# Pooled attention in front of two feed-forward stages: the order in which queries lie in the tiles, and when a pair's first queries are turned

## The chip, the cores and the metric

One Trainium2 chip, one core of it. Time is the device time of one execution in microseconds (us), lower is better; the runs give a median. A profile is one execution of the same program with the hardware profiler on.

## The reference, cut to what matters

```python
# q, k, v: (2 batches, 8 heads, 1152, 64) f32
q_pool = q.reshape(B, H, S // 2, 2, D).mean(axis=3)            # 576 queries a head
scores = matmul(q_pool, k.transpose(0, 1, 3, 2)) / sqrt(D)
attn = exp(scores - max(scores, -1)); attn /= attn.sum(-1) + 1e-9
x = matmul(attn, v)  ->  x of (1152 tokens, 512)                # token = batch * 576 + query
h = x @ w_in;  x = (h * tanh(softplus(h))) @ w_out              # 512 -> 2048 -> 512 ("Mish")
P = exp(x @ w_gate - max); 8 rounds: rows and columns of P scaled to sums (Sinkhorn)
out[n] = sum over 8 experts e of P[n, e] * (relu(x[n] @ w1[e]) @ w2[e])
```

Nothing after the attention mixes tokens except the column sums of P, which take all of them. So tokens may lie in any order on the chip, if the output rows go to their places.

## The kernel before, in words

Every matmul operand is split in two halves of fewer bits, a high and a low one (`split_hi`, L72, and `split_lo`, L80), and products are summed from them.

The attention goes over 8 pairs of heads (`p`), four in each batch. A pair has 2 x 576 = 1152 queries, 9 tiles of 128 (`QTL`): tiles 0 to 3 are of the first head, 5 to 8 of the second, and the middle tile 4 (`MID`) has the last 64 of the first head and the first 64 of the second. One step of the loop at L685 is one tile (`g`, with `t = g mod 9` inside pair `p`). In step `g` TensorE is given, in this order: the scores of tile `g` (`scores`, L443), one turning of keys if there is one, the turning of the exponentials of tile `g-3` (`transposes`, L521), up to 9 products of attention and values (`run_av`, L588), and the other turnings of keys or queries. ScalarE's exponential of tile `g` (`exps`, L462) stands after all of the step's copies.

- Scores come in one PSUM buffer. VectorE takes them to `e` (L458, three buffers), ScalarE makes the exponentials in place, and a DMA copies them to `er` (`hand_over`, L474, two buffers), issued in step `g+1`. TensorE turns them in step `g+3`. The buffer of `er` is free when tile `g-2` has been turned; the buffer of `e` when its copy has landed.
- Queries: `load_q` (L340) loads a pair's, `split_q` (L363) on GpSimd adds the two that are pooled, scales and splits them in four operations (`q0` to `q3`), `trans_q` (L428) turns four tiles at once, with the high half on partitions 0 to 63 and the low half on 64 to 127. ScalarE copies them to `qT`; `swap` (L423) makes a second copy with the two halves exchanged, by two DMAs inside SBUF. A tile's scores are two products for each third of the keys: with the first copy, then with the swapped one. The middle tile has its own buffers `qz` (`middle`, L403), with zeros where the other head's would be.
- `PREP` (L607) says in which `t` GpSimd does which split for pairs 1 and later (`PREP0` for pair 0): `q0` to `q3` of the next pair's queries; `k00`, `k01` the two halves of the next pair's first keys; `k10`, `k11` of its second; `v00` to `v11` of this pair's values. `TURN` (L612) says in which `t` the turnings stand: `"q": (7, 1, 2)` means that the next pair's tiles 0 to 3 are turned in step 7, its tiles 4 to 7 in its own step 1, tile 8 in its step 2.
- `loads` is a list of DMAs that a step adds to, and that SyncE issues at the start of the next step, in the order of the list and ahead of that step's `hand_over`. A swap gets onto it with its turning, a load of keys, values or queries when the last split of the ones before is put down, since the raw buffers are single.
- The row sums of a pair are turned, written to a row in DRAM and read back broadcast over the 64 partitions of each head (`turn_sums`, L485; `back` in step 4 of the next pair). GpSimd multiplies the attention's output `xs` by them and splits it (`split_x`, L575) at the end of that step 4, and `v10`, `v11`, `k10` and `k11` stand behind this on GpSimd.
- The attention's output is made in four groups of queries (`GROUPS`, L508: 256 and 320 of the first head, 320 and 256 of the second); `evac` (L561) adds its two halves into `xs`.

After the attention come the Mish stage, the gate, and the experts (`down`, L1175, sums into `oacc` by token tiles in the order `TILES`; in the last group each tile's rows go out by DMA, the last tile's in two halves of the columns).

Of the kernel before, what the change touches and what calls it, by code (L numbers as in the profile page):

```python
# [8 lines left out]
F32 = mybir.dt.float32  # L9
F32R = mybir.dt.float32r  # L10
# [3 lines left out]
AF = mybir.ActivationFunctionType  # L14
ALU = mybir.AluOpType
# [8 lines left out]
def pool_attention_mish_sinkhorn_kernel(  # L24
# [12 lines left out]
    nc = tc.nc  # L37
# [253 lines left out]
    with ExitStack() as actx:  # L291
# [48 lines left out]
        def load_q(p, part=slice(0, QTL)):  # L340
            b, hp, h0 = heads(p)
            if part.start == 0:
                raws["q", p] = q_p.tile([P, QTL, 2, D], F32, tag="qraw", name=f"qraw{p}")
            src = q[b, h0:h0 + 2].rearrange("h (s r) d -> (h s) r d", r=2)
            nc.sync.dma_start(
                out=raws["q", p][:, part], in_=src.rearrange("(t p) r d -> p t r d", p=P)[:, part])

        def split_kv(p, j, which, eng, part, more=True):
            if p == NPAIR:
# [46 lines left out]
        def q_tile(p, t):  # L396
            u, i = divmod(t, 4)
            if (p, u) not in qT:
                n = min(4, QTL - 4 * u)
                qT[p, u] = qt_p.tile([P, n, 2, P], F32R, tag=f"qT{n}", name=f"qT{p}_{u}", bufs=2)  # L400
            return qT[p, u], i

        def middle(p, ps, n):  # L403

            z = qz[p % 2]
            for j in range(2):
                nc.scalar.activation(
                    z[:, j, 0:n, j * D:(j + 1) * D], ps[:, 0:n, j * D:(j + 1) * D].bitcast(F32), AF.Copy)

        def trans_q0(u):  # L410

            n = min(2, QTL - 2 * u)
            ps = ps_t.tile([P, 2, 2, P], F32R, tag="t", name=f"psq0_{u}")
            for i in range(n):
                for s in range(2):
                    nc.tensor.transpose(
                        ps[:, i, s, :], qst[0][:, 2 * u + i, s:s + 2, :].rearrange("p a d -> p (a d)"), identr)
            t, i = q_tile(0, 2 * u)
            nc.scalar.activation(t[:, i:i + n], ps[:, 0:n].bitcast(F32), AF.Copy)
            if 2 * u <= MID < 2 * u + n:  # L420
                middle(0, ps[:, MID - 2 * u], 2)

        def swap(t):  # L423

            for a, b in ((0, D), (D, 0)):
                nc.sync.dma_start(out=t[a:a + D, :, 1, :].bitcast(F32), in_=t[b:b + D, :, 0, :].bitcast(F32))  # L426

        def trans_q(p, u):  # L428
            ps = ps_t.tile([P, 4, P], F32R, tag="t", name=f"psq{p}_{u}")
            t, _ = q_tile(p, 4 * u)  # L430
            n = min(4, QTL - 4 * u)
            for i in range(n):
                nc.tensor.transpose(
                    ps[:, i, :], qst[p][:, 4 * u + i, 0:2, :].rearrange("p a d -> p (a d)"), identr)
            nc.scalar.activation(t[:, :, 0, :], ps[:, 0:n].bitcast(F32), AF.Copy)
            loads.append(lambda: swap(t))
            if 4 * u == MID:
                middle(p, ps, 1)
                loads.append(lambda: swap(qz[p % 2]))
# [3 lines left out]
        def scores(g, pl=None):  # L443
            p, t = divmod(g, QTL)
            ps = (pl or ps_s).tile([P, 3, 512], F32, tag="s", name=f"psS{g}")
            for kb in range(3):
                if t == MID:
                    ops = [(qz[p % 2][:, j, s, :], kT[p, j]) for j in range(2) for s in range(2)]
                else:
                    x, i = q_tile(p, t)  # L450
                    ops = [(x[:, i, s, :], kT[p, int(t > MID)]) for s in range(2)]
                for n, (a, kt) in enumerate(ops):
                    nc.tensor.matmul(  # L453
                        ps[:, kb, 0:TH], lhsT=a, rhs=kt[:, kb * TH:(kb + 1) * TH],
                        start=(n == 0), stop=(n == len(ops) - 1))
            sc = e_p.tile([P, 3, TH], F32, tag="e", name=f"e{g}")
            nm = tiny.tile([P, 1], F32, tag="nm", name=f"nm{g}")
            nc.vector.tensor_scalar(  # L458
                sc, ps[:, :, 0:TH], -1.0, None, op0=ALU.mult, op1=ALU.min, accum_out=nm)
            scS[g] = (sc, nm)  # L460
# [24 lines left out]
        def turn_sums(p):  # L485

            ps = ps_t.tile([P, 4, P], F32, tag="t", name=f"psr{p}")
            nc.tensor.transpose(ps[0:QTL, 0, :], rsS.pop(p), ident)
            rt = rx_p.tile([QTL, P], F32, tag="rt", name=f"rt{p}")
            nc.vector.tensor_copy(rt, ps[0:QTL, 0, :])  # L490
            row = row_p.tile([QTL, P], F32, tag="row", name=f"row{p}")
            rx = rxS[p] = rx_p.tile([P, SQ], F32, tag="rx", name=f"rx{p}")

            def out():
                nc.sync.dma_start(out=row, in_=rt)
                loads.append(back)

            def back():
                flat = row.rearrange("t p -> (t p)")
                for j in range(2):  # L500
                    nc.sync.dma_start(
                        out=rx[j * D:(j + 1) * D, :], in_=flat[j * SQ:(j + 1) * SQ].unsqueeze(0).to_broadcast([D, SQ]))

            loads.append(out if p == NPAIR - 1 else lambda: loads.append(out))

# [42 lines left out]
        def queue_av(p, gi):  # L548
# [12 lines left out]
            def evac():  # L561
                ps = box["ps"]
                b, hp, h0 = heads(p)
                t = o_p.tile([D, SQ - c0], F32, tag="t", name=f"avt{p}_{gi}")
                nc.scalar.activation(t[:, 0:n], ps[D:2 * D, 0:n], AF.Copy)
                s = s0 - j * SQ
                if p not in xs_t:
                    xs_t[p] = xs_p.tile([P, SQ], F32, tag="xs", name=f"xs{p}")
                xs = xs_t[p]
                nc.vector.tensor_tensor(  # L570
                    out=xs[j * D:(j + 1) * D, s:s + n], in0=ps[0:D, 0:n], in1=t[:, 0:n], op=ALU.add)
                if gi == len(GROUPS) - 1:
                    late.append(lambda: split_x(p))

# [25 lines left out]
        for m in range(1, 2 * NG1 - 1):  # L600
# [4 lines left out]


        PREP = {  # L607
            "q0": 1, "q1": 2, "q2": 3, "q3": 4, "v00": 1, "v01": 2, "v10": 5, "v11": 7,
            "k00": 3, "k01": 4, "k10": 7, "k11": 8,
        }  # L610
        PREP0 = {"k00": 3, "k01": 3, "q0": 4, "q1": 4, "q2": 5, "q3": 5, "v10": 5, "v11": 7, "k10": 7, "k11": 8}
        TURN = {"k0": (5, 6, 7), "k1": (0, 2, 3), "k10": (0, 0, 2), "q0": (2, 2, 3), "q": (7, 1, 2)}  # L612

# [552 lines left out]
    up_t = ctx.enter_context(tc.tile_pool(name="up_t", bufs=1, side="right"))  # L1168
    wsum = ctx.enter_context(tc.tile_pool(name="wsum", bufs=1, side="right"))
    oacc = accp.tile([P, NTT, DM], F32, tag="acc", name="oacc")  # L1170
    TILES = [0, 1, 2, 6, 7, 8, 3, 4, 5]
    for j in range(NFC):
        wdt[-1, j] = tuple(y[:, j, :] for y in w2t[NG1])

    def down(g, t):  # L1175
# [4 lines left out]
        for si, (e, sl) in enumerate(segments(g)):  # L1180
            gate = Pm[:, t, e:e + 1]
            for j in range(parts):
# [17 lines left out]
                    nc.vector.scalar_tensor_tensor(  # L1200
                        out=oa, in0=ps[:, 0:w], scalar=gate, in1=oa, op0=ALU.mult, op1=ALU.add)
                if end and e == segments(g)[-1][0]:
                    nc.sync.dma_start(out=out[t * P:(t + 1) * P, cs], in_=oa)

    wslots = tuple(
        wpools[0].tile([P, 4, GF], F32R, tag="wu" + x, name=f"wslots{x}").rearrange(
# [81 lines left out]
```

## Time and profile before

| | |
|---|---|
| median of 3 runs | 1249.3 us (1243.05 to 1250.89) |
| profiled execution | 1245.79 us |
| its span, first to last instruction | 1244.0 us |
| TensorE busy | 1209.3 us, 97% of the span |
| VectorE, GpSimd, ScalarE busy | 852.2, 624.2, 593.6 us |

PE is TensorE's matmuls, PEld its weight loads, DVE VectorE, ACT ScalarE, POOL GpSimd, SP SyncE (which only issues DMAs). `L453` is line 453 of the kernel. `psS L453 <- DMA qT<-qT` reads: the matmuls that write `psS` at line 453 waited for the DMA from `qT` to `qT`. An engine that shows idle time before an instruction has this in brackets with what ended it.

### The profile page before, as it was taken

How to read it: one execution, taken by the hardware profiler on the slowest of the kernel's cores; microseconds unless marked ns; L12 is line 12 of the kernel's file. 1: busy time of each engine (PE TensorE's matmuls, PEld its weight loads, DVE VectorE, ACT ScalarE, POOL GpSimd, SP SyncE). 2: the span in 40 equal slices, each digit the busy share in tenths (PEclk: the TensorE clock that was granted, in tenths of full speed). 3: DMA queues.
4: the chain of work that ended last, by engine and by line, in shares of the span. 5: the costliest groups of instructions: out<-in, count | busy, mean ns of one | idle time of the engine just before them, and what ended most of it. 6: DMA issues, size and time to landing. Idle time of an engine off the chain costs nothing.

```text
span 1244.0 us, 19311 instructions
## 1 busy us (share of the span) xinstructions
PE 1209.3 (97%) x6840; PEld 1118.8 (90%) x6840; DVE 852.2 (69%) x1588; ACT 593.6 (48%) x1364; POOL 624.2 (50%) x704
## 2 busy tenths in 40 slices
PE   8988888999999999999999999999999999999998
PEld 8888888999999999988888999988888999998887
DVE  7777878895544433677876666866867767866865
ACT  7778878887644543452323333333323333333321
POOL 5346566423444333274756655555555664555552
PEclk9989999999999999999999999999999999999999
DMA  6766777754323220010111111111111111110112
GB/s 197 252 222 230 259 231 259 250 221 134 102 69 99 70 64 13 17 31 30 51 51 44 52 51 52 51 33 40 39 51 51 43 51 51 52 52 26 40 47 76
DMA packets 67552, 116.84 MB, mean 94 GB/s; under 512 B 7225, under 2 KB 39809, under 8 KB 67457
## 3 DMA queue, kind: packets, MB, share of 16 engines
q1 hardware_dynamic: 67456, 115.62, 29.0%
q8 instruction: 54, 0.88, 0.3%
q14 instruction: 42, 0.34, 0.1%
HBM read 66.86 MB, written 2.40 MB: 56 GB/s over the span
## 4 chain that ended last, share of the span: by engine, by line
PE 90%; DMA 5%; ACT 2%; DVE 1%; issue 1%; SPq 0%; POOL 0%; ACTq 0%; POOLq 0%; DVEq 0%
PE po L1192 30%; PE c L1034 25%; PE ph L224 10%; PE po L773 8%; PE psA L556 5%; PE psS L453 5%; PE psT L535 3%; DMA er<-e 3%; DMA qT<-qT 2%; ACT e L472 1%; ACT eth L538 1%; PE psk L391 1%; SPq L426 0%; PE psw L618 0%; PE pg L828 0%
## 5 line engine op out<-in xcount | busy, mean ns | idle before, releaser
L81 POOL TENSOR_TENSOR wslotsl<-s,wslotsh 128x256 fp32r<-128x256 f32 x180 | 132.5, 745 | 238.0 <-ACT wslotsh L74 238.0
L1200 DVE SCALAR_TENSOR_TENSOR oacc<-po,Pm,oacc 128x512 f32<-128x512 f32 (+1 forms) x217 | 161.0, 746 | 103.0 <-PE po L1192 96.8
L1192 PE MATMUL po<-wdbl,hhall 128*128 128x512 f32 (+1 forms) x543 | 214.4, 395 | 0.0
L1192 PE MATMUL po<-wdbh,hlall 128*128 128x512 f32 (+1 forms) x543 | 214.1, 394 | 0.0
L1192 PE MATMUL po<-wdbh,hhall 128*128 128x512 f32 (+1 forms) x543 | 214.0, 394 | 0.0
L1051 ACT ACTIVATE t<-c 128x384 f32<-128x384 f32 x80 | 39.2, 489 | 247.1 <-PE c L1034 247.1
L1071 ACT ACTIVATE hhall<-c 128x384 fp32r<-128x384 f32 x180 | 88.6, 492 | 129.0 <-DVE c L1067 126.3
L458 DVE TENSOR_SCALAR_CACHE_REDUCE e<-psS 128x1152 f32<-128x1152 f32 x72 | 97.4, 1353 | 40.0 <-PE psS L453 31.2
L1192 PEld LDWEIGHTS po<-wdbh,hhall 128*128 128x128 f32 x543 | 102.0, 188 | 24.4
L1192 PEld LDWEIGHTS po<-wdbl,hhall 128*128 128x128 f32 x543 | 102.0, 188 | 23.3
L1192 PEld LDWEIGHTS po<-wdbh,hlall 128*128 128x128 f32 x543 | 102.0, 188 | 23.3
L81 POOL TENSOR_TENSOR wslotsl<-rawu,wslotsh 128x256 fp32r<-128x256 f32 x120 | 91.0, 773 | 51.3 <-ACT wslotsh L74 51.3
L541 DVE TENSOR_TENSOR etl<-psT,eth 128x384 fp32r<-128x384 f32 (+1 forms) x240 | 108.1, 508 | 6.8 <-ACT eth L538 6.1
L453 PE MATMUL psS<-kT,qT 128*128 128x384 f32 x384 | 84.1, 352 | 20.5 <-DMA qT<-qT 17.1
L1072 DVE SCALAR_TENSOR_TENSOR hlall<-c,hhall 128x384 fp32r<-128x384 f32 x180 | 98.7, 548 | 2.1
L538 ACT ACTIVATE eth<-psT 128x384 fp32r<-128x384 f32 (+1 forms) x240 | 92.5, 477 | 11.4 <-PE psT L535 11.1
L1034 PE MATMUL c<-x2h,wslotsl 128*128 128x384 f32 x280 | 94.7, 338 | 0.0
L1034 PE MATMUL c<-x2h,wslotsh 128*128 128x384 f32 x280 | 94.5, 337 | 0.0
L1034 PE MATMUL c<-x2l,wslotsh 128*128 128x384 f32 x280 | 94.1, 336 | 0.0
L472 ACT ACTIVATE e<-e,nm 128x1152 f32<-128x1152 f32 x70 | 89.6, 1279 | 0.0
L453 PEld LDWEIGHTS psS<-kT,qT 128*128 128x128 f32 x384 | 66.2, 193 | 24.5 <-issue 12.2
L74 ACT ACTIVATE wslotsh<-s 128x256 fp32r<-128x256 f32 x180 | 72.0, 410 | 24.3 <-DVE s L1000 24.3
(358 smaller groups left out, 3074.3 us busy)
## 6 DMA issues: line engine op xcount, KB each, us to landing
er<-e SPq DMA_DIRECT2D x70, 576.0 KB, 3.5
rawd<-in_moe_w_dram SPq DMA_DIRECT2D x60, 256.0 KB, 2.8
rawu<-in_moe_w_dram SPq DMA_DIRECT2D x30, 384.0 KB, 3.2
raw<-in_moe_w_in_dram SPq DMA_DIRECT2D x16, 512.0 KB, 4.3
raw<-in_moe_w_out_dram SPq DMA_DIRECT2D x16, 512.0 KB, 3.6
vraw<-in_v_dram SPq DMA_DIRECT2D x16, 288.0 KB, 3.3
kraw<-in_k_dram SPq DMA_DIRECT2D x15, 288.0 KB, 4.1
qraw<-in_q_dram SPq DMA_DIRECT2D x7, 576.0 KB, 6.9
```

What stands on the lines that cost most here:

```text
L81: eng.tensor_tensor(out=lo, in0=src, in1=hi.bitcast(F32), op=ALU.subtract)
L224: nc.tensor.matmul(ps[:, 0:TH], lhsT=a, rhs=b, start=(n == 0), stop=(n == len(ops) - 1))
L453: nc.tensor.matmul(ps[:, kb, 0:TH], lhsT=a, rhs=kt[:, kb * TH:(kb + 1) * TH], start=(n == 0), stop=(n == len(ops) - 1))
L458: nc.vector.tensor_scalar(sc, ps[:, :, 0:TH], -1.0, None, op0=ALU.mult, op1=ALU.min, accum_out=nm)
L472: nc.scalar.activation(e, sc, AF.Exp, bias=nm, scale=-1.0, accum_out=rsS[p][:, t:t + 1])
L538: nc.scalar.activation(eh[:, cs, o:o + b - a], ps[:, 0:3, a:b], AF.Copy)
L541: nc.vector.tensor_tensor(out=el[:, cs, o:o + b - a], in0=ps[:, 0:3, a:b], in1=eh[:, cs, o:o + b - a].bitcast(F32), op=ALU.subtract)
L773: nc.tensor.matmul(ps[:, 0:TH], lhsT=a, rhs=b, start=(n == 0), stop=(n == len(ops) - 1))
L1034: nc.tensor.matmul(cb[c], lhsT=a_, rhs=b_, start=FIRST[n] and m == 0, stop=LAST[n] and m == len(ops) - 1, skip_group_check=True)
L1072: los.append(lambda: nc.vector.scalar_tensor_tensor(out=lo, in0=b, scalar=0.0, in1=hi.bitcast(F32), op0=ALU.max, op1=ALU.subtract))
L1192: nc.tensor.matmul(ps[:, 0:w], lhsT=a, rhs=b[:, cs], start=(n == 0), stop=(n == len(ops) - 1))
L1200: nc.vector.scalar_tensor_tensor(out=oa, in0=ps[:, 0:w], scalar=gate, in1=oa, op0=ALU.mult, op1=ALU.add)
```

## The change

- A head's first 512 queries are loaded four consecutive ones to a partition (2 KB in one piece), so that tile `t` has queries 4p + t; the last 64 of each head fill the middle tile. One load of a pair's queries becomes four, pair 0's last part three in place of one.
- The second head's middle queries now come last in its order, so `evac` writes the third group in two pieces (64 and 256 columns), and the row sums come back in three pieces in place of two.
- `qT` and `qz` have the exchanged copy in a half of their own, so that each side of a swap is one run in a partition.
- The tokens keep this order to the end. A tile's output rows are written four rows apart (`token_rows`); tiles that hold parts of two runs go out in two transfers, 15 transfers in place of 10. The last tile is now tile 3, which is one run.
- In `PREP`, `v11` moves from 7 to 6, `k00` from 3 to 2, `k01` from 4 to 3; in `TURN`, the first queries' turning moves from 7 to 6. `PREP0` stays.

```diff
@@ load_q
-            src = q[b, h0:h0 + 2].rearrange("h (s r) d -> (h s) r d", r=2)
-            nc.sync.dma_start(
-                out=raws["q", p][:, part], in_=src.rearrange("(t p) r d -> p t r d", p=P)[:, part])
+            for j in range(2):
+                t0 = j * (MID + 1)
+                ts = slice(max(part.start, t0), min(part.stop, t0 + MID))
+                if ts.start < ts.stop:
+                    src = q[b, h0 + j, 0:2 * MID * P].rearrange("(p t r) d -> p t r d", t=MID, r=2)
+                    nc.sync.dma_start(out=raws["q", p][:, ts], in_=src[:, ts.start - t0:ts.stop - t0])
+                if part.start <= MID < part.stop:
+                    nc.sync.dma_start(
+                        out=raws["q", p][j * D:(j + 1) * D, MID],
+                        in_=q[b, h0 + j, 2 * MID * P:S].rearrange("(p r) d -> p r d", r=2))
@@ q_tile, swap, scores
-                qT[p, u] = qt_p.tile([P, n, 2, P], F32R, tag=f"qT{n}", name=f"qT{p}_{u}", bufs=2)
+                qT[p, u] = qt_p.tile([P, 2, n, P], F32R, tag=f"qT{n}", name=f"qT{p}_{u}", bufs=2)
...
-                nc.sync.dma_start(out=t[a:a + D, :, 1, :].bitcast(F32), in_=t[b:b + D, :, 0, :].bitcast(F32))
+                nc.sync.dma_start(out=t[a:a + D, 1].bitcast(F32), in_=t[b:b + D, 0].bitcast(F32))
...
-                    ops = [(x[:, i, s, :], kT[p, int(t > MID)]) for s in range(2)]
+                    ops = [(x[:, s, i, :], kT[p, int(t > MID)]) for s in range(2)]
@@ turn_sums, back
-                for j in range(2):
+                for j, x, a, n in ((0, 0, 0, SQ), (1, 0, SQ + D, SQ - D), (1, SQ - D, SQ, D)):
                     nc.sync.dma_start(
-                        out=rx[j * D:(j + 1) * D, :], in_=flat[j * SQ:(j + 1) * SQ].unsqueeze(0).to_broadcast([D, SQ]))
+                        out=rx[j * D:(j + 1) * D, x:x + n], in_=flat[a:a + n].unsqueeze(0).to_broadcast([D, n]))
@@ evac
-                nc.vector.tensor_tensor(
-                    out=xs[j * D:(j + 1) * D, s:s + n], in0=ps[0:D, 0:n], in1=t[:, 0:n], op=ALU.add)
+                a = max(0, -s)
+                for s, a, b in ((SQ - D, 0, a), (s + a, a, n)):
+                    if a < b:
+                        nc.vector.tensor_tensor(
+                            out=xs[j * D:(j + 1) * D, s:s + b - a], in0=ps[0:D, a:b], in1=t[:, a:b], op=ALU.add)
@@ PREP, TURN
-            "q0": 1, "q1": 2, "q2": 3, "q3": 4, "v00": 1, "v01": 2, "v10": 5, "v11": 7,
-            "k00": 3, "k01": 4, "k10": 7, "k11": 8,
+            "q0": 1, "q1": 2, "q2": 3, "q3": 4, "v00": 1, "v01": 2, "v10": 5, "v11": 6,
+            "k00": 2, "k01": 3, "k10": 7, "k11": 8,
...
-        TURN = {"k0": (5, 6, 7), "k1": (0, 2, 3), "k10": (0, 0, 2), "q0": (2, 2, 3), "q": (7, 1, 2)}
+        TURN = {"k0": (5, 6, 7), "k1": (0, 2, 3), "k10": (0, 0, 2), "q0": (2, 2, 3), "q": (6, 1, 2)}
@@ TILES, down
-    TILES = [0, 1, 2, 6, 7, 8, 3, 4, 5]
+    TILES = [0, 1, 2, 6, 7, 8, 4, 5, 3]
...
-                    nc.sync.dma_start(out=out[t * P:(t + 1) * P, cs], in_=oa)
+                    for rows, to in token_rows(t):
+                        nc.sync.dma_start(out=out[to, cs], in_=oa[rows])
```

## Rows read from the trace of the kernel before

**Rows 1.** The page: engines' busy us; TensorE's and DMA's busy tenths in 40 slices.
```profile
PE 1209.3 (97%) x6840; PEld 1118.8 (90%) x6840; DVE 852.2 (69%) x1588; ACT 593.6 (48%) x1364; POOL 624.2 (50%) x704
...
PE   8988888999999999999999999999999999999998
...
DMA  6766777754323220010111111111111111110112
```

**Rows 2.** Busy us by stretch: PE, PEld, DVE, ACT, POOL; clock, DMA share, GB/s.
```profile
109.00:135.00 26.00, 26.00 (x200) 25.61 (x201) 22.58 (x46) 20.67 (x47) 9.67 (x10) 0.94 0.76 253
...
295.00:464.00 169.00, 169.00 (x962) 169.00 (x962) 74.76 (x134) 90.29 (x180) 71.64 (x55) 1.00 0.28 85
```

**Rows 3.** Who waited for whom: us in total, times, longest.
```profile
PE psS L453 <- DMA qT<-qT: 17.1, 7, 3.5
...
DVE e L458 <- DMA er<-e: 7.7, 6, 2.0
...
PE psT L535 <- DMA er<-e: 6.4, 6, 1.7
```

**Rows 4.** The chain of waits, seam of pairs 3 and 4: start, us, what.
```profile
130.04 6.39 DMA er<-e
...
139.68 4.13 DMA qT<-qT
```

**Rows 5.** Stretches at half clock, the longest of four and the sum.
```profile
71.10:77.92 6.82, 6.18 (x28) 6.12 (x29) 2.96 (x6) 1.77 (x5) 1.35 (x1) 0.50 0.44 167
...
sum 17.08, PE 16.15 PEld 15.92 DVE 9.48 ACT 5.88 POOL 2.57; mean PE 4.04 PEld 3.98 DVE 2.37 ACT 1.47 POOL 0.64
```

**Rows 6.** Timeline of SyncE's issues, 134 to 142: start, us, engine, line.
```profile
137.59 0.47 SPq L478 DMA_DIRECT2D er<-e  x1
138.14 0.54 SPq L337 DMA_DIRECT2D vraw<-in_v_dram  x1
138.99 1.35 SPq L426 DMA_DIRECT2D qT<-qT  x2
```

**Rows 7.** Timeline of GpSimd, 129 to 142; v11 is the vst row.
```profile
130.31 1.44 POOL L579 TENSOR_TENSOR xs<-xs,rx 128x576 f32<-128x576 f32 x1 [5.10 <-DMA rx<-row]
...
136.03 0.62 POOL L78 TENSOR_SCALAR wuh<-wt 128x512 fp32r<-128x512 f32 x1
136.61 1.43 POOL L81 TENSOR_TENSOR vst<-vraw,vst 128x576 fp32r<-128x576 f32 x1
```

**Rows 8.** DMA packets of 130.6 to 131.9 (queries) and 134.2 to 135.4 (er).
```profile
DMA packets 749, 0.40 MB, mean 308 GB/s; under 512 B 7, under 2 KB 747, under 8 KB 748
...
DMA packets 127, 0.50 MB, mean 419 GB/s; under 512 B 16, under 2 KB 16, under 8 KB 127
```

**Rows 9.** Timeline of TensorE, the first scores of pair 4.
```profile
141.26 0.34 PE L453 MATMUL psS<-kT,qT 128*128 128x384 f32 x1
143.94 1.12 PE L453 MATMUL psS<-kT,qT 128*128 128x384 f32 x5 [2.35 <-DMA qT<-qT]
```

**Rows 10.** Timeline of GpSimd at the seam of pairs 1 and 2.
```profile
63.38 1.41 POOL L81 TENSOR_TENSOR vst<-vraw,vst 128x576 fp32r<-128x576 f32 x1
```

**Rows 11.** Timeline of SyncE's issues, 126.8 to 131.
```profile
127.46 0.54 SPq L345 DMA_DIRECT2D qraw<-in_q_dram  x1
128.10 1.13 SPq L337 DMA_DIRECT2D kraw<-in_k_dram  x1
```

**Rows 12.** DMA issues of the page: KB each, us to landing.
```profile
er<-e SPq DMA_DIRECT2D x70, 576.0 KB, 3.5
```

**Rows 13.** Timeline of ScalarE, exponential of tile 6 and copy of queries.
```profile
134.65 1.25 ACT L472 ACTIVATE e<-e,nm 128x1152 f32<-128x1152 f32 x1
...
138.31 0.66 ACT L435 ACTIVATE qT<-psq 128x512 fp32r<-128x512 f32 x1
```

**Rows 14.** Line 570, VectorE's sum: ns min/median/max, first and last start.
```profile
L570 DVE TENSOR_TENSOR xs<-psA,avt x32: 404/445/485, 28.0 to 290.8; 64x256 f32<-64x256 f32 x16, 64x320 f32<-64x320 f32 x16
```

**Rows 15.** Line 1203, output transfers: ns to issue, first and last start.
```profile
L1203 SPq DMA_DIRECT2D out_dram<-oacc x10: 332/332/343, 1224.9 to 1241.4; - x10
```

More of the change, by code (lines that the diff above doesn't have):

```diff
@@ L407, in middle @@
                 nc.scalar.activation(
-                    z[:, j, 0:n, j * D:(j + 1) * D], ps[:, 0:n, j * D:(j + 1) * D].bitcast(F32), AF.Copy)
+                    z[:, 0:n, j, j * D:(j + 1) * D], ps[:, 0:n, j * D:(j + 1) * D].bitcast(F32), AF.Copy)
         def trans_q0(u):
@@ L418, in trans_q0 @@
             t, i = q_tile(0, 2 * u)
-            nc.scalar.activation(t[:, i:i + n], ps[:, 0:n].bitcast(F32), AF.Copy)
+            nc.scalar.activation(
+                t[:, :, i:i + n].rearrange("p s n q -> p n s q"), ps[:, 0:n].bitcast(F32), AF.Copy)
             if 2 * u <= MID < 2 * u + n:
@@ L434, in trans_q @@
                     ps[:, i, :], qst[p][:, 4 * u + i, 0:2, :].rearrange("p a d -> p (a d)"), identr)
-            nc.scalar.activation(t[:, :, 0, :], ps[:, 0:n].bitcast(F32), AF.Copy)
+            nc.scalar.activation(t[:, 0], ps[:, 0:n].bitcast(F32), AF.Copy)
             loads.append(lambda: swap(t))
@@ L447, in scores @@
                 if t == MID:
-                    ops = [(qz[p % 2][:, j, s, :], kT[p, j]) for j in range(2) for s in range(2)]
+                    ops = [(qz[p % 2][:, s, j, :], kT[p, j]) for j in range(2) for s in range(2)]
                 else:
                     x, i = q_tile(p, t)
-                    ops = [(x[:, i, s, :], kT[p, int(t > MID)]) for s in range(2)]
+                    ops = [(x[:, s, i, :], kT[p, int(t > MID)]) for s in range(2)]
                 for n, (a, kt) in enumerate(ops):
@@ L565, in evac @@
                 nc.scalar.activation(t[:, 0:n], ps[D:2 * D, 0:n], AF.Copy)
-                s = s0 - j * SQ
+                s = s0 - j * (SQ + D)
                 if p not in xs_t:
@@ L1170, in pool_attention_mish_sinkhorn_kernel, with token_rows @@
     oacc = accp.tile([P, NTT, DM], F32, tag="acc", name="oacc")
-    TILES = [0, 1, 2, 6, 7, 8, 3, 4, 5]
+    TILES = [0, 1, 2, 6, 7, 8, 4, 5, 3]
+    def token_rows(t):
+        cuts = sorted({0, P} | {x - t * P for b in range(B) for x in range(b * SQ, (b + 1) * SQ + 1, P)
+                                if 0 < x - t * P < P} | {x * SQ - t * P for x in range(B) if 0 < x * SQ - t * P < P})
+        for a, z in zip(cuts, cuts[1:]):
+            b, i = divmod(t * P + a, SQ)
+            if i < MID * P:
+                r = b * SQ + i % P * MID + i // P
+                yield slice(a, z), slice(r, r + (z - a - 1) * MID + 1, MID)
+            else:
+                yield slice(a, z), slice(b * SQ + i, b * SQ + i + z - a)
     for j in range(NFC):
```

## The prediction, made before any run of the changed kernel

> **What bounds the kernel now.** I read the page first. TensorE is busy for 1209.3 of 1244.0 us, but the slices are not alike: the first eight or so read 8, with DMA engines busy too, and the rest read 9 [rows 1]. The table by stretch says the same closer up: 109 to 135 us, the middle of a head pair, has TensorE busy 26.00 of 26.00 us, and so has everything from 295 to 464 us [rows 2]. So a gain can only come from the seams between the eight pairs, where the new pair's queries are turned. The waits of TensorE there have two names: 17.1 us in seven pieces for the swapped halves of qT, and 6.4 us in six pieces for er, the exponentials that a DMA carries over; VectorE waits for the same er 7.7 us [rows 3]. The chain of waits orders them at the seam of pairs 3 and 4: one er issued at 130.04 takes 6.39 us to land, the turning follows, the swap issued at 139.68 takes 4.13 us, and TensorE's scores stand behind it [rows 4]. Two things hang on this: the late er (tile 4's) holds tile 7, the late swap holds the next pair's first scores.
>
> A third loss follows the seams. In four stretches, 17.08 us together, the granted clock was 0.50 (1.2 instead of 2.4 GHz); TensorE was busy 16.15 us in them [rows 5]. Each begins within 1.2 us of the end of a seam's wait. Work at half clock takes double, so they cost 16.15 / 2 = 8.1 us.
>
> **The change, part by part.** *First queries turned in step 6.* Their swap joins the DMA queue's list one step earlier. Nothing is added in sum: four transposes and one copy of 0.66 us move from step 7 to step 6. The queries have long been split by then. But SyncE takes its list in order, and the change also moves the values' low half (v11) to step 6, so the next values' load now stands in step 7 ahead of the two swaps, and tile 6's er behind them. That load may overwrite the values only when GpSimd has finished v11. Before, the order was er at 137.59, values at 138.14, swaps from 138.99 [rows 6]. When will v11 end? GpSimd works without a gap from 130.31, when the row sums have landed; v11 runs from 136.61 to 138.04 behind one weight copy of 0.62 us [rows 7]. With v11 a step earlier that copy comes after it: end at 138.04 - 0.62 = 137.4. Then values load 137.5, swaps at 138.05 and 138.6, er at 139.2. The swap's 4.13 us held a wait behind that er; er's 0.59 MB at 419 GB/s is 1.4 us of queue [rows 8], so 2.7 us are left and the swap lands at 141.3 instead of 143.8. TensorE gets to the first scores at 141.26 [rows 9], a little earlier by what comes below, so 0.5 us of 2.35 us remain. At seams whose weight work is lighter v11 ends sooner than the step needs: at the seam of pairs 1 and 2 it ends at 64.8 [rows 10] and nothing remains. Pair 0 has its own table, where v11 is not moved, and its swap comes out free. I take 16 of the 17.1 us; bounds 7 (one us a seam, the issue times' difference alone) and 17.1.
>
> *Half clock.* Rows show that three of seven seams kept the full clock although their waits were as long (141.26 to 143.94 is one), so the rows don't say when it falls, only that it fell at the end of a wait each time. If the waits go I take 7 of the 8.1 us; bounds 0 and 8.1. The Trainium skill, "TensorE: Matmul & The Clock Gate", section "HAM oscillation — how this bites in real kernels", says that waits for DMA between bursts of matmuls bring the clock to half and that work kept dense stays at full rate; by it all 8.1 us come back, and the sum would be 1.1 us lower. The four stretches at 0.50 agree, the three seams without one don't.
>
> *Queries four to a partition.* One load of 1152 pieces of 512 bytes becomes four: two of 128 pieces of 2 KB, two of 64 of 512 bytes. In the queue 512-byte pieces ran at 308 GB/s and 4608-byte pieces at 419 [rows 8]. No row has a full queue of 2 KB pieces, so the 0.59 MB take between 1.9 us (no gain) and 0.52 / 0.419 + 0.07 / 0.308 = 1.5 us. I take 1.5, since the pieces are four times longer. The queue is served in order and tile 4's er stands right behind, so that er lands 0.4 us earlier at each of the six waits of [rows 3], 2.4 us; bounds 0 and 6.4. Moving the first keys' split up a step (k00, k01) puts the second keys' load ahead of the queries' but does not shorten the queue before that er. The Trainium skill, "DMA: Bandwidth & Descriptors", section "Why small descriptors are slow (HBM only)", gives about 3 cycles of overhead a packet: 19 cycles for 512 bytes against 67 for 2 KB, an estimate of 12% saved, where the rows at 308 and 419 allow 24%. By the page the term would be 1.2 us instead of 2.4. It also says that copies inside SBUF don't pay for short pieces, so the swaps in whole halves would gain nothing; I had put them at nothing.
>
> Issuing four loads takes 4 x 0.6 = 2.4 us of SyncE, against 0.54 + 1.13 us for queries and keys [rows 11]: from 127.46 to 129.9, and er follows at 130.04 [rows 4]. It fits with 0.1 us to spare; without cover it costs up to 0.7 us a seam.
>
> *What is added.* (1) Tile 6's er goes out at 139.2 instead of 137.59. At 3.5 us to land [rows 12] it is there at 142.7; TensorE comes to it after the first scores (1.1 us) and a key turn, at 142.8. I put 1.5 us for all seams; bounds 0 and 7 x 1.6 = 11. (2) The copy of 0.66 us now stands before tile 6's exponential on ScalarE instead of tile 7's [rows 13]; the exponential is done at 136.6 instead of 135.9, and SyncE is held until 137.4 anyway: 0, at most 5. (3) VectorE's sum is cut in two for one group per pair: 8 more instructions under 0.45 us [rows 14] on an engine with 3.4 us free in 26 [rows 2]: 0, at most 3. (4) The row sums come back in three pieces instead of two, one more issue of 0.6 us; what waits is GpSimd, and v11 with it: 0, at most 0.6 a seam. (5) Five more output transfers: issues of 0.3 us where tiles come some 2 us apart, and the last tile still has two transfers, of 1 KB pieces, the last of them at the end [rows 15]: 0, within 0.5 either way. (6) At the start, two more issues ahead of the first values' load; they are needed 10 us later: 0, at most 1.
>
> Sum: -16 - 7 - 2.4 + 1.5 = -23.9 us. The profiled execution took 1245.8 us, so 1221.9; it was 3.5 us below the median of the runs, 1249.3, which makes 1225.4. I say **1225**.
>
> **The rivals.** *Only the wait for the swaps goes.* The seams still show er's wait, and the clock falls there as before: 1249.3 - 16 = 1233 us. For it: DMA engines are full over the seam, and er's lateness is not touched by the earlier turning. Against: what is left is a wait of 1 to 2 us instead of 3 to 4.
>
> *SyncE is held by the values' load.* The swaps go out only 1 us sooner, because GpSimd has no gap before v11 [rows 7], and they land 1 us sooner: 7 us off, and 2.4 for the queries: 1240 us. For it: the worked seam has little room. Against: at 64.8 there was room, and er is no longer ahead of the swaps.
>
> *Slower, by the same queue.* Values' load, both swaps and tile 6's er stand in one line behind GpSimd's v11, and that behind the row sums' broadcast, which has a piece more. The swap lands 3.9 us after v11 ends, so it comes even with before when v11 ends at 139.9, 2.5 us later than I worked out; from there each us costs a us at each seam, and er, 1.7 us after v11, pays too. At 4.5 us late the seams lose 2 us each: 1249.3 + 14 = 1263 us. For it: the broadcast lands in a full queue, and keys now follow it at once. Against: keys are issued behind it, and the queue is served in order.
>
> *More than the listed waits goes* (a calmer queue helps er as well): 1245.8 - 17.1 - 8.1 - 6.4 = 1214 and below.
>
> **How the numbers follow.** The forecast has 0.62 (its own range 1215 to 1233), only the swaps 0.17, the held SyncE 0.12, slower 0.05, more 0.04. The range that leaves out no more than two in ten goes from 1214 to 1240. About 1% (12.5 us, 1236.8 to 1261.8) is what a measurement of this kernel tells from no change: faster is 0.62 + 0.17 + 0.04 = 0.83, the same 0.12, slower 0.05.
>
> **What would show it.** Right: TensorE's wait for qT falls from 17.1 to 1 or 2 us; no stretch at 0.50 after the first 10 us, or one; er's wait 3 to 5 us; the pairs 3 us shorter each, and the part from the Mish stage on as long as before. The values' load in step 7 is seen waiting for GpSimd's vst, with the swaps right behind it. Wrong: TensorE's wait only changes its name, to er or to kst; swaps that land more than 3 us after their issue; the stretches at 0.50 still there; a last transfer that lands later than 2 us after its issue.

## The result and the profile after

The changed kernel takes 1230.8 us, the median of four runs (1229.7 to 1234.2). Four runs of the kernel before, beside them, have a median of 1246.8 us. The ratio is 0.9876, with a 95% interval of 0.9834 to 0.9918: a gain of 10 to 21 us, of which 16 is the middle. The forecast was a gain of 24. The time lies inside the range and 6 us above the value named.

The profiled execution took 1231.0 us, its span 1229.0. First its page, with the lines that answer to [rows 1], TensorE's granted clock in 40 slices, and the packets.

```profile
PE 1204.5 (98%) x6840; PEld 1113.0 (91%) x6840; DVE 856.7 (70%) x1596; ACT 593.8 (48%) x1364; POOL 623.2 (51%) x704
...
PE   8999999999999999999999999999999999999998
...
PEclk9999999999999999999999999999999999999999
DMA packets 56352, 116.85 MB, mean 95 GB/s; under 512 B 8312, under 2 KB 24896, under 8 KB 56256
```

The early slices of TensorE now read 9 where [rows 1] read 8; packets fell from 67552 to 56352 at the same bytes. TensorE is busy 4.8 us less than before, and its mean granted clock over the span is 1.000 (0.993 before). The same instructions in less busy time is what the end of the half-clock stretches of [rows 5] looks like.

Next, the table of who waited for whom (us in total, times, longest), the lines that answer to [rows 3].

```profile
DVE e L466 <- DMA er<-e: 10.5, 7, 2.7
...
PE psS L461 <- DMA qT<-qT: 6.4, 6, 1.9
PE psS L461 <- DVE e L466: 6.1, 10, 1.5
...
PE psT L543 <- DMA er<-e: 3.4, 6, 1.3
```

The wait for the swapped queries is down from 17.1 us to 6.4, but it is still there at six seams. TensorE's wait for er went from 6.4 to 3.4; VectorE's went the other way, from 7.7 to 10.5, but a second execution of the same kernel has 4.6 there (e11). And TensorE now waits 6.1 us, in ten pieces, for VectorE to empty psS. Before, that was 2.7 us in three pieces.

The line of the attention's exponential on ScalarE (ns, first and last start) says which part of the kernel became shorter. First the kernel before, then the changed one.

```profile
L472 ACT ACTIVATE e<-e,nm x70: 1245/1279/1341, 13.4 to 276.3; 128x1152 f32<-128x1152 f32 x70
```

```profile
L480 ACT ACTIVATE e<-e,nm x70: 1245/1277/1337, 13.5 to 260.2; 128x1152 f32<-128x1152 f32 x70
```

The last exponential starts 16.1 us sooner. From there to the end it takes 967.7 us before and 968.8 after, so the whole gain lies in the head pairs. The stretch that answers to the second line of [rows 2] is unchanged in kind: TensorE without a gap, at full clock.

```profile
285.00:454.00 169.00, 169.00 (x963) 169.00 (x962) 72.78 (x132) 89.04 (x176) 70.11 (x54) 1.00 0.28 84
```

Now one seam closer up, that of pairs 3 and 4, the one the forecast worked out. First the timeline of SyncE's issues (start, us), which answers to [rows 6].

```profile
127.06 0.33 SPq L337 DMA_DIRECT2D vraw<-in_v_dram  x1
127.44 1.12 SPq L434 DMA_DIRECT2D qT<-qT  x2
128.75 1.47 SPq L486 DMA_DIRECT2D er<-e  x2
```

Then the timeline of GpSimd, which answers to [rows 7]. The row of 1.43 us on vst is v11.

```profile
120.01 1.44 POOL L590 TENSOR_TENSOR xs<-xs,rx 128x576 f32<-128x576 f32 x1 [6.04 <-DMA rx<-row]
...
125.60 1.43 POOL L81 TENSOR_TENSOR vst<-vraw,vst 128x576 fp32r<-128x576 f32 x1
```

Then the first scores of pair 4 on TensorE, which answer to [rows 9].

```profile
130.58 0.34 PE L461 MATMUL psS<-kT,qT 128*128 128x384 f32 x1
132.02 1.12 PE L461 MATMUL psS<-kT,qT 128*128 128x384 f32 x5 [1.10 <-DMA qT<-qT]
```

And the chain of waits there (start, us, what), which answers to [rows 4].

```profile
120.01 5.76 DMA er<-e
...
127.98 3.91 DMA qT<-qT
```

This is the picture the forecast had drawn: GpSimd starts on the row sums only when they land, v11 follows and ends at 125.60 + 1.43 = 127.03, and the values' load leaves SyncE at 127.06, with the swaps behind it and two er's behind the swaps. The sizes differ. The second swap, issued at 127.98, needs 3.91 us, not 2.7. TensorE was ready at 130.58 and waits 1.10 us, not 0.5. The seam of pairs 1 and 2, where nothing was to remain, has a wait of 0.32 us; the longest is 1.91.

### The profile page after: what moved, and what is told of

Same layout as the page of the kernel before. It is cut to its first block, busy times and chain, and to the rows that moved or that the text cites. A ratio compares the mean times of both kernels' runs of the same rounds, so it can differ in the third digit from the quotient of the medians.

```text
span 1229.0 us, 19413 instructions
## 1 busy us (share of the span) xinstructions
PE 1204.5 (98%) x6840; PEld 1113.0 (91%) x6840; DVE 856.7 (70%) x1596; ACT 593.8 (48%) x1364; POOL 623.2 (51%) x704
## 2 busy tenths in 40 slices
DMA packets 56352, 116.85 MB, mean 95 GB/s; under 512 B 8312, under 2 KB 24896, under 8 KB 56256
## 4 chain that ended last, share of the span: by engine, by line
PE 90%; DMA 4%; DVE 3%; ACT 1%; issue 1%; POOL 0%; ACTq 0%; DVEq 0%; POOLq 0%; SPq 0%
PE po L1215 30%; PE c L1045 26%; PE ph L224 10%; PE po L784 8%; PE psS L461 5%; PE psA L564 4%; DMA er<-e 3%; PE psT L543 3%; DVE e L466 2%; DMA qT<-qT 1%; DVE etl L549 1%; PE psk L398 1%; ACT eth L546 0%; ACT e L480 0%; PE psw L629 0%
## 5 line engine op out<-in xcount | busy, mean ns | idle before, releaser
L466 DVE TENSOR_SCALAR_CACHE_REDUCE e<-psS 128x1152 f32<-128x1152 f32 x72 | 97.3, 1352 | 23.8 <-DMA er<-e 10.5
L564 PE MATMUL psA<-etl,vst 128*128 128x256 f32 (+1 forms) x288 | 80.4, 303 | 0.5 <-DVE rs L490 0.5
```

Of the source, the lines that this page charges most:

```text
L466: nc.vector.tensor_scalar(sc, ps[:, :, 0:TH], -1.0, None, op0=ALU.mult, op1=ALU.min, accum_out=nm)
L564: nc.tensor.matmul(box["ps"][:, 0:n], lhsT=vst[p, j][:, c].rearrange("p a d -> p (a d)"), rhs=(el, eh)[which][:, c, 0:n], start=(c == 0 an ...
```

## The experiments

Theory A, before the first runs: the early turn takes the swaps' wait away, and what the changed kernel doesn't gain is lost because the values' low half, moved to step 6 as well, puts the next values' load ahead of the swaps on SyncE, where it waits for GpSimd. Its rivals stand in the expectations.

**One number of the change alone (e1).** The kernel before, with only the first queries' turn moved.

```diff
-        TURN = {"k0": (5, 6, 7), "k1": (0, 2, 3), "k10": (0, 0, 2), "q0": (2, 2, 3), "q": (7, 1, 2)}
+        TURN = {"k0": (5, 6, 7), "k1": (0, 2, 3), "k10": (0, 0, 2), "q0": (2, 2, 3), "q": (6, 1, 2)}
```

> The kernel before with one edit: TURN's first queries in step 6. Theory A (the gain comes from the earlier turning, and the values' load put ahead of the swaps takes a part of it back): TensorE's wait for qT is under 3 us instead of 17.1, no stretch at half clock, 1246.8 - 15 - 8 = about 1224 us, 5 to 7 us faster than the changed kernel. Theory B (loads in 2 KB pieces and swaps in whole halves carry much of the gain): the wait for qT stays above 6.4 us and the time is 1236 us or more.

It took 1222.8 us (1222.5 to 1223.7), ratio 0.9776 (0.9750 to 0.9801). That is 8 us less than the whole change. Who waited for whom in it:

```profile
DVE e L458 <- DMA er<-e: 8.2, 7, 2.0
...
PE psS L453 <- DVE e L458: 6.3, 11, 1.5
PE psT L535 <- DMA er<-e: 5.3, 7, 1.4
```

No wait of TensorE for qT is left in the table at all. The wait for VectorE is there, 6.3 us, as in the changed kernel: it comes with the early turn, not with the layout. TensorE's wait for er falls by only 1.1 us without the new layout.

**The layout alone (e2).** The changed kernel with the old step numbers.

```diff
-            "q0": 1, "q1": 2, "q2": 3, "q3": 4, "v00": 1, "v01": 2, "v10": 5, "v11": 6,
-            "k00": 2, "k01": 3, "k10": 7, "k11": 8,
+            "q0": 1, "q1": 2, "q2": 3, "q3": 4, "v00": 1, "v01": 2, "v10": 5, "v11": 7,
+            "k00": 3, "k01": 4, "k10": 7, "k11": 8,
...
-        TURN = {"k0": (5, 6, 7), "k1": (0, 2, 3), "k10": (0, 0, 2), "q0": (2, 2, 3), "q": (6, 1, 2)}
+        TURN = {"k0": (5, 6, 7), "k1": (0, 2, 3), "k10": (0, 0, 2), "q0": (2, 2, 3), "q": (7, 1, 2)}
```

> The changed kernel with PREP and TURN as before: the load of four queries to a partition, the token order and the swaps in whole halves alone. Theory A: wait for qT 15 to 17 us, half-clock stretches of 10 to 17 us in sum, time 1243 to 1247 us. Theory B: wait for qT under 12 us and 1238 us or less.

1240.0 us (1237.1 to 1242.4), ratio 0.9911 (0.9880 to 0.9941). The rows of its waits:

```profile
PE psS L461 <- DMA qT<-qT: 14.2, 7, 2.6
...
DVE e L466 <- DMA er<-e: 5.6, 6, 1.3
...
PE psT L543 <- DMA er<-e: 4.2, 6, 1.1
```

Neither theory had it quite. The layout is worth 7 to 15 us by itself, more than the 2.4 the forecast gave it, and part of that is 2.9 us less wait for the swaps, where the forecast had nothing. Which half of the layout does that is e5's question.

**The values' low half back in step 7 (e3).** The changed kernel, one number put back.

```diff
-            "q0": 1, "q1": 2, "q2": 3, "q3": 4, "v00": 1, "v01": 2, "v10": 5, "v11": 6,
+            "q0": 1, "q1": 2, "q2": 3, "q3": 4, "v00": 1, "v01": 2, "v10": 5, "v11": 7,
```

> The changed kernel with v11 back in step 7, so that the next values' load follows the swaps and tile 6's er instead of standing ahead of them. Theory A (SyncE held by GpSimd's v11 is what is left of the wait): wait for qT falls from 6.4 to 1.5 us or less, tile 6's er goes out 1 to 1.5 us earlier, time about 1225 us. Rival C (the swaps land late because the DMA queue is full, whatever stands ahead on SyncE): wait for qT stays at 5 to 7 us, time 1230 to 1232 us.

1221.4 us (1220.6 to 1222.1), ratio 0.9763 (0.9732 to 0.9793): 9 us under the changed kernel, and the fastest of all that ran. Its waits:

```profile
PE psS L461 <- DVE e L466: 6.1, 10, 1.5
...
DVE e L466 <- DMA er<-e: 5.3, 5, 1.7
...
PE psT L543 <- DMA er<-e: 2.9, 4, 1.4
```

And its SyncE at the seam of pairs 3 and 4:

```profile
123.22 1.12 SPq L434 DMA_DIRECT2D qT<-qT  x2
125.07 0.48 SPq L486 DMA_DIRECT2D er<-e  x1
126.07 0.34 SPq L337 DMA_DIRECT2D vraw<-in_v_dram  x1
```

Swaps, er, values: the order is turned round, and the swaps leave 2.85 us before the values' load instead of 0.38 us after it. TensorE no longer waits for them.

The swaps need ScalarE's copy of the turned queries. Its row (start, us) at this seam says how long SyncE held them: first the changed kernel, then e3.

```profile
124.36 0.60 ACT L443 ACTIVATE qT<-psq 128x512 fp32r<-128x512 f32 x1
```

```profile
122.59 0.60 ACT L443 ACTIVATE qT<-psq 128x512 fp32r<-128x512 f32 x1
```

In e3 the swaps leave 0.03 us after the copy has ended (123.19), in the changed kernel 2.48 us after it (124.96). At the six seams where the changed kernel waits, this hold is 1.2 to 2.6 us and TensorE's wait 0.3 to 1.9 us, at each seam shorter than the hold. Had the swaps left with the copy and needed the same time to land, TensorE would not have waited.

**The keys' split put back (e4).**

```diff
-            "k00": 2, "k01": 3, "k10": 7, "k11": 8,
+            "k00": 3, "k01": 4, "k10": 7, "k11": 8,
```

> The changed kernel with k00 and k01 back in steps 3 and 4, so that the second keys' load stands behind the four loads of queries, not ahead. Theory A (the queue ahead of tile 4's er holds the same bytes either way): within 2 us of the changed kernel, 1229 to 1233 us. Rival D (SyncE issues keys after 2.4 us of queries, so tile 4's er goes out 0.5 us later at each seam): 3 to 4 us slower, 1234 us or more, with VectorE's wait for er above 12 us instead of 10.5.

1229.7 us (1227.8 to 1232.1), with TensorE waiting 6.3 us for qT and 3.5 for er: the changed kernel again. This part of the change shows no effect, in either direction.

**The swaps in whole halves alone (e5).** The kernel before with only the queries' turned tile laid out by halves, so that a swap moves one run of 2 KB a partition instead of four of 512 bytes. (The copies into it and the scores index it to match; the zero-padded tile of the middle block, qz, likewise.)

```diff
-                qT[p, u] = qt_p.tile([P, n, 2, P], F32R, tag=f"qT{n}", name=f"qT{p}_{u}", bufs=2)
+                qT[p, u] = qt_p.tile([P, 2, n, P], F32R, tag=f"qT{n}", name=f"qT{p}_{u}", bufs=2)
...
-                nc.sync.dma_start(out=t[a:a + D, :, 1, :].bitcast(F32), in_=t[b:b + D, :, 0, :].bitcast(F32))
+                nc.sync.dma_start(out=t[a:a + D, 1].bitcast(F32), in_=t[b:b + D, 0].bitcast(F32))
```

> The kernel before with the layout of qT and qz alone: each side of a swap is one run of a partition (2 KB, 1 KB or 512 bytes) instead of pieces of 512 bytes; queries loaded as before. What the prediction put at nothing. Theory A (the pieces of a swap don't matter, the 1240 us of the layout run come from the queries' load): wait for qT 16 to 18 us, time within 4 us of the kernel before, 1245 to 1252 us. Rival E (the swaps' shorter issue and transfer bring the layout's gain): wait for qT 14 to 15 us and 1240 to 1243 us.

1238.8 us (1237.8 to 1239.5), ratio 0.9935 (0.9911 to 0.9960). Its waits:

```profile
PE psS L454 <- DMA qT<-qT: 14.1, 7, 2.6
...
DVE e L459 <- DMA er<-e: 7.3, 6, 1.6
PE psT L536 <- DMA er<-e: 6.0, 6, 1.4
```

The 3.0 us less wait for the swaps are all here. The chain of waits says where they come from: the step from a swap's issue to its landing, at the seams of pairs 1 and 2, 2 and 3, and 3 and 4. First the kernel before (its third is in [rows 4], 4.13 us), then e5.

```profile
67.22 4.38 DMA qT<-qT
...
104.40 4.40 DMA qT<-qT
```

```profile
67.13 3.65 DMA qT<-qT
...
100.23 3.86 DMA qT<-qT
...
135.33 4.00 DMA qT<-qT
```

A mean of 4.30 us before and 3.84 here, 0.47 us less a seam; the table of waits gives 3.0 / 7 = 0.43. (In e2 the same three steps have a mean of 3.96 us.) And the wait is shorter at each of the seven seams, in e5 as in e2. So the rival of this run's theory, by which short pieces cost inside SBUF too, held; the time came out 1.2 us under its range. The other half of the layout, the queries' load, is what e2 has and e5 has not: the waits for er, 6.0 and 7.3 us here, are 4.2 and 5.6 there. But e2 isn't faster than e5 (1240.0 and 1238.8 us, in different sets of runs), so those 1.8 us of TensorE's wait can't be found in the time.

**GpSimd's order kept, the values' load one step later on SyncE (e6).** This parts two readings of e3: that GpSimd's work in step 6 costs something by itself, or only the load's place on SyncE.

```diff
-                    loads.append(lambda: load_kv(p, j, which))
+                    one = lambda: load_kv(p, j, which)
+                    loads.append((lambda: loads.append(one)) if which == "v" and j == 0 and p > 1 else one)
```

> The changed kernel with v11 left in step 6 on GpSimd, and only the values' load that follows it kept back one step on SyncE, behind the swaps and tile 6's er. Theory A (the load's place on SyncE is what costs): wait for qT 1 us or less, 1221 to 1223 us, like the run with v11 back in step 7. Rival F (GpSimd's order with v11 in step 6 is what costs, through keys or weights that come later): wait for qT still above 4 us or a new wait for kst, 1228 to 1231 us.

1222.6 us, ratio 0.9804 (0.9780 to 0.9828); three of its four runs took 1221.2 to 1222.7. The fourth took 2349.3 us at full clock; what happened in it was not found. Its SyncE at the same seam:

```profile
122.03 1.12 SPq L435 DMA_DIRECT2D qT<-qT  x2
123.94 0.48 SPq L487 DMA_DIRECT2D er<-e  x1
124.54 0.52 SPq L337 DMA_DIRECT2D vraw<-in_v_dram  x1
```

TensorE has no wait for qT here, with v11 still in step 6. So 8 us hang on the load's place on SyncE, and none that the runs show on GpSimd's order.

**Only the swaps put first (e9).** The changed kernel, with the first queries' swaps placed at the head of SyncE's list. The values' load and tile 6's er stay in their order behind them.

```diff
-            loads.append(lambda: swap(t))
+            loads.insert(0, lambda: swap(t)) if u == 0 else loads.append(lambda: swap(t))
```

> The changed kernel with the first queries' swaps put at the head of SyncE's list for step 7, ahead of the values' load; the load still waits there for GpSimd, and tile 6's er still stands behind it. It parts the two things that the load holds up. If the late swap alone costs: wait for qT 1 us or less and 1221 to 1223 us. If the late er of tile 6 costs too: wait for qT 1 us or less, but waits for er 3 us or more above those of the run with v11 in step 7, and 1225 to 1228 us.

1223.0 us (1219.9 to 1225.4), ratio 0.9809 (0.9781 to 0.9837). Its SyncE:

```profile
123.41 1.12 SPq L434 DMA_DIRECT2D qT<-qT  x2
125.53 0.34 SPq L337 DMA_DIRECT2D vraw<-in_v_dram  x1
126.37 2.15 SPq L486 DMA_DIRECT2D er<-e  x2
```

The swaps' wait is gone from TensorE's table; its wait for er is 4.3 us, against 3.4 in e6 and 2.9 in e3, where tile 6's er leaves ahead of the values' load. By these rows that er's late start costs 0.9 to 1.4 us, hardly more than the 1.1 us by which two executions of the changed kernel differ in the same row (3.4, and 2.3 in e11). The late swaps are the rest. Whether a swap is late because SyncE is held, or because the values' bytes are ahead of it in the queue, this run doesn't part: it takes away both. The hold is enough by itself (e3, above); what the bytes alone would cost isn't shown.

**What is left: can er come sooner?** Two runs on top of e3. One theory (G) puts er's remaining wait down to the expert weights' first loads, which fall on the seam, another (I) to the next queries' load. The rival of both (H): the queue is full there, and moving bytes only moves the wait. e8 sends the first weight chunk's loads two steps sooner (one of them leaves SyncE at 71.19 us instead of 78.84):

```diff
-            at(ts[0] - 2.4 * stage, "dma", dma)
+            at(ts[0] - (3.4 if busy else 2.4) * stage, "dma", dma)
```

> The changed kernel with v11 back in step 7 and, besides, the loads of the first weight chunk (512 KB, one in each of pairs 1 to 4) issued two steps earlier, out of the queue ahead of tile 4's er. Theory G (tile 4's er lands late by what stands ahead of it in the full queue, and 1.2 us of that are the weights): VectorE's wait for er falls from 5.3 to 2 us or less and TensorE's from 2.9 to 1 us or less, time 1217 to 1219 us. Rival H (the queue is full either way, the bytes only move within it): waits for er as they were, 1220 to 1223 us.

1223.0 us (1222.5 to 1223.7); TensorE waits 4.7 us for er instead of 2.9. Nothing gained. e10 sends the next queries' load two steps later:

```diff
-                    loads.append(lambda: load_q(p + 1))
+                    one = lambda: load_q(p + 1)
+                    two = lambda: loads.append(one)
+                    loads.append((lambda: loads.append(two)) if p else one)
```

> The changed kernel with v11 back in step 7 and, from pair 1 on, the next pair's queries loaded two steps later (step 7 instead of 5), so that tile 4's er has no queries ahead of it in the queue; GpSimd needs them only in the next pair. Theory I (tile 4's er is late by the 1.5 us that the queries take right ahead of it): waits for er fall from 5.3 (VectorE) and 2.9 us (TensorE) to 2 us or less together, time 1217 to 1219 us. Rival H (the bytes only move within a full queue, another er is late instead): waits for er within 2 us of these, 1220 to 1224 us.

1224.2 us (1221.1 to 1228.0). Its waits:

```profile
PE psT L545 <- DMA er<-e: 4.1, 4, 2.4
...
PE psS L463 <- DMA qT<-qT: 2.9, 5, 0.8
```

The swaps' wait is back, 2.9 us, and er's did not fall. So G and I failed. H is the nearest, though TensorE's wait for er rose by 1.8 and 1.2 us, and the second time lies just over H's range.

**The changed kernel once more (e11),** on the chip and beside the runs of e10.

> The changed kernel unaltered, beside the run above on one chip: 1229 to 1233 us, as at the first time, if chip and day make no difference to the comparison of the runs with the changed kernel.

1230.6 us (1229.4 to 1231.6), ratio 0.9882 (0.9821 to 0.9943). So the 8 to 9 us between it and e1, e3, e6 and e9 are no matter of the chip or the hour. The kernel before had medians of 1251.2, 1245.7 and 1245.6 us beside the three sets. The rows of its waits show how far two executions of one kernel differ:

```profile
PE psS L461 <- DMA qT<-qT: 7.2, 6, 2.0
...
DVE e L466 <- DMA er<-e: 4.6, 5, 1.4
...
PE psT L543 <- DMA er<-e: 2.3, 5, 1.1
```

In the first execution these were 6.4, 10.5 and 3.4. A difference of about 1 us in one row of TensorE's waits says little, and VectorE's row says less.

## Why the prediction was right, and where its size was off

**Direction and place: right.** What bound the kernel was the seams, the wait for swapped queries was the largest loss in them, and most of the clock came back with it. The parts that were put at nothing (the sum cut in two, the row sums in three pieces, the output's rows) cost little: the part behind the last exponential takes 967.8 to 968.8 us in the kernels with the new layout and 967.2 to 967.7 in those with the old one (before, e1, e5). What the difference of up to a us is lost to isn't shown; the longer wait for the column sums, 1.9 us here, is 0.9 in e11, the same kernel, and in e2, e3, e6 and e9.

**The step that failed** is the swap term: "the swap's 4.13 us held a wait behind that er; er's 0.59 MB at 419 GB/s is 1.4 us of queue, so 2.7 us are left", and with it "0.5 us of 2.35 us remain" and nothing at the other seams. The order on SyncE was foreseen to the row, and so was the hold: v11 ends 7.0 us after GpSimd starts on the row sums, and 7.1 us after it in the forecast. The time to landing wasn't. The second swap needed 4.02, 4.43 and 3.91 us at the first three of these seams (the chain; above for the third), hardly less than the 4.38, 4.40 and 4.13 before. Swaps that land more than 3 us after their issue were one of the forecast's own signs of being wrong. The median from issue to landing over all swaps is 3.2 us in the changed kernel and 2.5 in e3. So 6.4 us remained, not about 1, and the term was 17.1 - 6.4 = 10.7 us instead of 16.

Why er's absence saved so little can be read at the seam of pairs 3 and 4. First a stretch before and one in the changed kernel in which no data moved (the last two numbers, DMA share and GB/s); data move from its end on.

```profile
137.40:138.70 1.30, 1.18 (x10) 1.04 (x9) 1.30 (x6) 1.30 (x6) 1.30 (x3) 1.00 0.00 0
```

```profile
126.75:128.00 1.25, 0.77 (x5) 0.70 (x5) 1.25 (x6) 1.25 (x7) 1.25 (x3) 1.00 0.00 0
```

Before, er went out at 137.59, and data moved 1.1 us later. The values' load stood ahead of the swaps then, too [rows 6], and the second swap was issued 1.0 us after the first data. Now the load is the first, issued at 127.06; data move 0.9 us later, and the second swap is issued at that very moment. From the first data to that swap's landing it took 5.1 us before (138.70 to 143.81) and takes 3.9 now (128.00 to 131.89): 1.2 us less, not far from er's 1.4. But counted from the swap's own issue only 0.2 us are saved, for the swap is now issued 1.0 us earlier in this sequence. The forecast took er's bytes off a time that it counted from that issue, and left out the load's start, which the swap now waits out. Its own rival, the held SyncE, had the mechanism, but priced it at 7 us saved of the swaps' wait and 1240 us; the truth lay between.

Term by term, for the changed kernel and for e3, in which the failed step is taken out (us, from the tables of waits and the busy time of TensorE; half clock as the fall of its busy time):

| term | forecast | changed kernel | e3 |
|---|---|---|---|
| wait for qT | -16 | 17.1 to 6.4: -10.7 | -17.1 |
| half clock | -7 | 1209.3 to 1204.5: -4.8 | to 1203.0: -6.3 |
| TensorE's wait for er | -2.4, +1.5 | 6.4 to 3.4: -3.0 | to 2.9: -3.5 |
| TensorE's wait for VectorE (psS) | not named | 2.7 to 6.1: +3.4 | +3.4 |
| wait for the column sums | not named | 0.9 to 1.9: +1.0 | 0 |
| sum | -23.9 | -14.1 | -23.5 |
| profiled execution, from 1245.8 | 1221.9 | 1231.0: -14.8 | 1221.3: -24.5 |

The forecast's sum is e3's time, to 0.6 us: what was worked out is the change with the load kept out of the swaps' way. That the sum agrees so well is partly luck. TensorE's wait for er fell by 3.5 us where the two terms make 0.9, and the wait for VectorE, which no term named, took 3.4 back. In e11's execution the rows of the changed kernel are -9.9, -3.5, -4.1, +3.3 and 0, so the +1.0 for the column sums is one execution's.

**Right for partly wrong reasons.** Three smaller steps were off and nearly cancel.
- *What is late next.* In step 7 the four turnings stood between the turning of er and the pair's last scores (0.51 us from 137.34 in the kernel before, with the scores at 137.97). With them gone, TensorE comes to these scores half a us before VectorE has emptied psS, once a pair: 3.4 us more that the forecast didn't name, since it let the move of the turnings cost nothing. The row at the seam of pairs 3 and 4 in the changed kernel:

```profile
127.31 1.32 PE L461 MATMUL psS<-kT,qT 128*128 128x384 f32 x6 [0.48 <-DVE e L466]
```

These waits appear in every kernel with the early turn (6.1 to 6.5 us in e1, e3, e6, e8, e9, e10) and not in e2 and e5 (2.7).
- *Swaps in whole halves at nothing.* In e5 they are worth 3.0 us of wait and, with the clock, 5 to 11 us of time by the interval. With the early turn they cover nothing that is still waited for: e1 has no wait for qT without them. The forecast had leaned on the Trainium skill, "DMA: Bandwidth & Descriptors", section "Why small descriptors are slow (HBM only)", by which transfers inside SBUF don't suffer from short pieces. e5 doesn't agree: 0.47 us sooner a swap.
- *Queries four to a partition, 2.4 us.* e2 beside e5 shows the waits for er fall by 1.8 and 1.7 us, about the size, but not in the time there; e3 beside e1, both with the early turn and on one chip, shows 2.4 us less of TensorE's wait for er (5.3 to 2.9) and 1.4 us less time (their runs don't overlap, the intervals of their ratios do; e3 also has the swaps in whole halves and the keys' split a step earlier). In the queue, a stretch of 2 KB and 512-byte pieces ran at 364 GB/s, between the 308 and 419 of [rows 8]:

```profile
DMA packets 360, 0.55 MB, mean 364 GB/s; under 512 B 50, under 2 KB 134, under 8 KB 359
```

Tile 6's late er, put at 1.5 us, costs 0.9 to 1.4 by e9's rows. That doesn't speak against the term, but two executions of one kernel differ by almost as much.

**Half clock.** Of 8.1 us the busy time shows 4.8 in the changed kernel and 6.3 in e3, both with a mean granted clock of 1.000. So no half-clock time is left in these two executions, and the difference between their busy times, 1.5 us, has another source, which was not looked for. The Trainium skill, "TensorE: Matmul & The Clock Gate", section "HAM oscillation — how this bites in real kernels", has dense work stay at full rate; in e3, with no wait for the swaps, the rows agree. The changed kernel is not free of it: in e11 a stretch at 0.50 follows the wait for the swaps that ended at 133.49, of 1.94 us. In e1, whose swaps are on time, one is left, after a wait of 1.44 us for er that ended at 187.23. First e11's row, then e1's:

```profile
133.53:136.94 3.41, 3.41 (x18) 3.32 (x19) 1.49 (x4) 1.15 (x4) 2.92 (x5) 0.50 0.48 163
```

```profile
188.85:192.26 3.41, 3.41 (x17) 3.31 (x17) 2.78 (x9) 3.20 (x8) 3.41 (x4) 0.50 0.76 262
```

One reading of the forecast was wrong: that three of the seven seams before kept the full clock "although their waits were as long". Their waits are the three shortest, 0.92, 2.35 and 2.39 us; the four that lost it had waited 2.61 to 3.52. But length alone doesn't sort the seams: in e5 a wait of 2.63 us kept the clock.

**Open.** What would shorten er's remaining wait isn't settled: e8 and e10 moved transfers within the seam and gained nothing, and fewer bytes there, or a second values buffer so that the load need not wait for v11, weren't tried. Nor is it shown what the values' bytes ahead of a swap cost without SyncE's hold, which is enough to explain the waits.

## What to carry to other kernels

When a transfer is moved up on an engine that issues in order, write down the engine's whole new order and price what stands ahead of it, with its bytes and with the wait it carries: here a load that waits for GpSimd, standing ahead of the swaps instead of behind them, cost 8 to 9 us, and putting any one of the three (load, swap, GpSimd's step) elsewhere gave them back. When a transfer leaves the place ahead of another, don't take its whole time off: what is issued first in its stead has a start of its own, 0.9 us here. And try a bundle's edits one by one: one number of this change, alone, beats all of it.

## What the runs showed of the hardware that was not expected

*Short pieces cost inside SBUF as well.* 128 KB moved as runs of 2 KB landed after a mean of 3.84 us, as runs of 512 bytes after 4.30 (three seams each, above, with er and the values' load ahead of them); two issues took 1.28 us instead of 1.35 on SyncE at the seam of pairs 3 and 4.

*The kernel before is uneven, and its clock with it.* Its 21 runs beside the experiments spread from 1238.7 us, with a mean granted clock of 0.996, to 1255.4 us, with 0.985. A straight line through them gives 0.47 us of time for each us at half clock (twice the missing share of the clock, times the span; correlation 0.81): about the half that work at half speed must cost. The kernels without a seam wait for the swaps ran at 0.998 to 1.000, and e1 and e3 spread by 1.1 and 1.5 us. But e9, at 0.999 to 1.000 and without that wait, still spread by 5.6 us, so the clock is not all of the scatter. Taking the wait away bought the wait and most of the clock.
